# A four-segment attention block with FFN on one core: values of segment 0 in column strips, its first FFN matmul in 64-row tiles, segment 2's FFN in general PSUM banks, VectorE products split off

## Chip, cores and metric

The kernel runs on one core of a Trainium2 chip. The metric is device time in microseconds (us) of one execution; a time is the median of several runs. The engines are TensorE (PE; its weight loads are listed apart as PEld), VectorE (DVE), ScalarE (ACT), GpSimd (POOL) and SyncE (SP), which issues nearly all DMAs. Each has its own queue and runs it in order.

## The reference, cut to what matters

```python
# x: [1, 2048, 576] bf16; 32 heads of 18; N = 4 segments of L = 512; F = 4608
h  = x + A(layernorm(x))
h2 = h + gelu(layernorm(h) @ w1 + b1) @ w2 + b2

def A(x):
    q, k, v = x @ wq, x @ wk, x @ wv            # split in heads and segments
    M, z = 0, 0
    for s in range(4):
        p     = softmax(qs @ ks.T * scale + mask)
        a_dot = p @ vs
        a_mem = phi(qs) @ M / (phi(qs) @ z + 1e-6)
        outs.append(g * a_mem + (1 - g) * a_dot)  # g = sigmoid(beta), per head
        M += phi(ks).T @ vs ;  z += sum(phi(ks))
    return concat(outs) @ wo
```

In segment 0 the memory is still empty, so only the softmax part is computed there. `mask` adds -1e9 (in bf16) where `ar[:, None] < ar[None, :]`; the kernel sets those weights to nought after the exponential.

## The kernel before, in words

**Order.** The program is a list of about 1,740 small operations ("ops"). Each has a name made of a stage tag and a kind (`A1exp`, `C00F1`), the engine it runs on, and a place in one overall order: both come from the table `TIMETABLE`, in which a row such as `"A00exp": "a 94 113"` says that the two ops of that name go to ScalarE at places 94 and 113 (letters p, a, d, g, s for TensorE, ScalarE, VectorE, GpSimd, SyncE). `schedule()` sorts the ops by place and gives buffers out in that order; so the order of every engine's queue, that of the DMAs on SyncE among them, is written out by hand. The costs in `add(...)` only choose which buffer of a pool is taken.

**Stages.** For each segment s of 512 tokens (4 tiles of 128):
- X: load x, layernorm (`layernorm`: statistics on VectorE, the power -0.5 on GpSimd, subtract and scale on VectorE), transpose. Segment 0 is transposed by TensorE, the others are written to `xnd` in DRAM and read back by a transposing DMA ("flip").
- P: projections q, k, v in halves of 288 columns into one PSUM bank each, evicted by VectorE or ScalarE ("copy"); q and k go to DRAM (`qkst`) and come back transposed (`A0flip`, `A1flip`, ...).
- M: the memory update (`M`, `macc`, `mblk`).
- A: scores in four 32-row tiles (`st0` in segment 0, `st` in the others) into `st`, the single score buffer of four banks; one exponential of 128x2048 on ScalarE (`exp`); masks on VectorE or GpSimd; values (`val`). In segments 1 to 3 the value matmul has v (19 columns) as its stationary operand in column strips of 32, the weights streaming, and the result is turned by VectorE (`valT`), divided (`comb`) and added to the memory part (`mem`, `memT`, `memfin`, `comb2`); `oT` turns the sum for the output projection. In segment 0 (`stage_A0`, lines 885 to 993) the value matmul has the weights `pt` as stationary operand (128x128) and v streaming, 19 columns each; the result has tokens on partitions, is divided in `comb`, brought into the order of the output projection by GpSimd (`perm`), and turned by TensorE (`T`) for tiles 0 and 1, by a DMA for tiles 2 and 3.
- B: output projection (`Po`), residual (`hadd`), second layernorm, transposed again into `x2T` (`B00T`, `B01T` on TensorE for the first two tiles of segment 0, DMA for all others).
- C: first FFN matmul (`F1`), bias, gelu. D: second FFN matmul (`F2`), residual, output.

**The first FFN matmul.** In segments 1 to 3 the contraction of 576 is cut into nine blocks of 64 rows; two row tiles of the array work side by side on two outputs, and `xn2` carries a copy of its first 64 columns behind its end (`tail`), so that the odd blocks can be transposed too. In segment 0 the contraction is cut into five blocks of 128 (the last one of 65, whose last row is one and carries the bias), over 256 tokens at a time (`C00`, `C01`), two outputs to a PSUM bank. Segments 0 and 1 evict to `hT` and then apply the gelu in batches; segments 2 and 3 (`s >= DIRECT`, which is 2) use four banks of their own, `late_s`, that come free when the score buffer is closed, and ScalarE applies the gelu straight from PSUM, one output at a time (line 1192).

**Buffers.** Four general PSUM banks `c_s` serve projections, values, transposes, F1 of segments 0 and 1 and all of F2. `x2T` of segments 1 to 3 is one buffer, `xd_s`, that lies over the two buffers of `xT_s`.

Of the kernel before, what the change touches and what calls it, by code (L numbers as in the profile page):

```python
# [24 lines left out]
    "A00T": "p 172",  # L25
    "A00comb": "d 142 148",
    "A00copy": "d 177",
    "A00exp": "a 94 113",
    "A00mask": "g 114 105 124 136",
    "A00perm": "g 155",  # L30
    "A00st0": "p 88 107",
    "A00val": "p 137 140 143 144",
    "A01T": "p 233",
    "A01comb": "d 181 220",
    "A01copy": "d 240",
    "A01exp": "a 134 151 174 198",
    "A01mask": "d154 g146 g182 g196",
    "A01perm": "g 229",
    "A01st0": "p 129 147 170 190",
    "A01val": "p 158 159 163 164 199 210 216 208",  # L40
    "A02comb": "d 406 466",
    "A02dma": "s 477",
    "A02exp": "a 343 370 358 383 429 397",
    "A02mask": "g 362 371 405 396",
    "A02perm": "g 470",
    "A02st0": "p 340 366 353 380 423 394",
    "A02val": "p 369 377 379 402 372 373 420 430 460 464 446 421",
    "A03comb": "d 322 351",
    "A03dma": "s 386",
    "A03exp": "a 239 269 254 224 286 328 298 312",  # L50
    "A03flip": "s 518",
    "A03mask": "g 249 257 293 303",
    "A03opad": "g 545",
    "A03perm": "g 355",
    "A03st0": "p 235 265 251 218 282 325 295 308",
    "A03val": "p 258 274 314 281 263 275 271 278 311 341 347 339 348 323 333 326",
    "A0flip": "s 96 85 127 119 184 192 202 231",
    "A1comb": "d 555 589 673 686 740 764 817 846",
    "A1comb2": "g570 g640 g680 g720 g744 d779 g820 g850",
    "A1eg": "a 445 475 565 652 581 696 710 768",  # L60
    "A1exp": "a 452 482 468 544 496 568 586 601 623 638 656 689 678 703 731 721 776 791 822 758",
    "A1flip": "s 417 426 503 527 495 542 600 716",
    "A1mask": "g512 g514 g499 g489 g553 g562 g506 g513 g618 g602 g612 g624 g660 g647 g648 g663 d707 g705 g697 g702 g708 g728 g748 g738 g774 g809 d785 g801 "
        "d819 d836 g769 d793",
    "A1mem": "p 517 532 655 692 617 759 733 780",
    "A1memT": "d 521 534 659 709 622 761 743 823",
    "A1memfin": "d 564 636 677 714 690 762 790 838",
    "A1oT": "d 695 799 826 858 856",
    "A1pq": "d 459 485 632 665 590 747 719 777",
    "A1rg": "g 438 449 548 604 556 711 682 750",  # L70
    "A1st": "p 447 478 465 530 492 563 582 595 614 634 651 687 670 698 727 717 770 786 812 751",
    "A1val": "p 528 579 631 674 712 753 810 840",
    "A1valT": "d 538 584 654 684 725 757 813 844",
    "A2comb": "d 947 998 984 1028 1049 1078 1135 1159",
    "A2comb2": "g951 d1013 g988 g1040 d1057 d1085 g1138 g1160",
    "A2eg": "a 835 784 907 954 999 985 1042 1058",
    "A2exp": "a 863 842 876 853 899 930 946 915 961 975 990 1015 1026 1006 1046 1064 1074 1104 1089 1132",
    "A2flip": "s 797 658 816 804 948 890 1025 970",
    "A2mask": "g881 d848 g854 g886 g896 g916 g919 g908 d950 d955 g963 d938 g935 g972 d987 g992 g1007 g1034 d1024 g1030 g1033 g1062 g1051 g1052 d1111 g1109 "
        "g1080 d1113 g1140 g1097 g1144 g1148",  # L80
    "A2mem": "p 845 855 952 981 1039 1016 1073 1103",
    "A2memT": "d 852 864 959 997 1048 1019 1076 1106",
    "A2memfin": "d 893 965 979 1009 1054 1079 1128 1139",
    "A2oT": "d 1043 1117 1095 1168 1169",
    "A2pq": "d 841 829 941 962 1003 1011 1060 1087",
    "A2rg": "g 828 825 891 832 968 995 1044 1055",
    "A2st": "p 860 839 872 849 892 927 942 910 957 971 986 1012 1022 1004 1035 1059 1072 1100 1081 1122",
    "A2val": "p 894 925 967 1001 1041 1069 1124 1150",
    "A2valT": "d 900 994 973 1021 1047 1077 1127 1155",
    "A3comb": "d 1221 1253 1299 1323 1374 1388 1416 1427",  # L90
    "A3comb2": "g1225 g1257 d1309 d1332 g1377 g1392 d1422 d1429",
    "A3eg": "a 1096 1170 1226 1161 1290 1337 1351 1370",
    "A3exp": "a 1146 1157 1167 1175 1231 1254 1269 1210 1295 1281 1319 1307 1329 1343 1355 1365 1375 1384 1396 1411",
    "A3flip": "s 1002 1133 1094 1107 1230 1166 1296 1301",
    "A3mask": "d1158 g1165 d1180 g1176 g1171 g1239 g1235 g1243 d1270 d1283 g1277 d1245 g1249 g1303 d1292 g1308 g1325 g1320 d1335 d1339 g1338 d1363 g1366 "
        "g1361 d1371 g1397 d1391 d1399 g1402 g1412 g1419 d1420",
    "A3mem": "p 1145 1224 1247 1276 1310 1347 1390 1389",
    "A3memT": "d 1147 1228 1258 1279 1311 1359 1407 1394",
# [186 lines left out]
    "omg": "g 81",  # L285
    "ones": "a 213 166",
    "tri": "g 66",
    "warm": "p 5 14 20 24",
    "x1": "a 2",
}  # L290

# [109 lines left out]
def kernel(  # L401
# [13 lines left out]
    P = 128  # L415
# [1035 lines left out]
```

## Time and profile before

| | us |
|---|---|
| median of 3 runs (lowest, highest) | 457.35 (456.49, 458.07) |
| the profiled execution | 457.92 |
| its span, first to last instruction | 456.2 |
| granted clock of TensorE | 1.00 |

The profile lists busy time by engine, then by source line. A duration there runs from an instruction's start to its modelled end; neighbours on one engine overlap, so the time that one takes from its engine is read from one start to the next. "1276 PE MATMUL" is the second FFN matmul, 1187 the row-tiled first one, 1225 that of segment 0, 754 the projections, 919 and 944 scores and values of segment 0, 1048 and 1074 those of segments 1 to 3.

```profile
L1187 PE MATMUL ps_l<-xreg,w1g 64*128 64x512 bf16 x648 | 70.5, 376 | 0.0
L1225 PE MATMUL ps_c<-xreg,w1g 128*128 128x256 bf16 x288 | 40.9, 272 | 0.3 <-DMA w1g<-in_B_w_dram 0.3
L944 PE MATMUL ps_c<-v_aug,pt 128*128 128x19 bf16 x320 | 12.2, 172 | 0.2
L1074 PE MATMUL ps_c<-pt,v_aug 128*19 128x512 bf16 x96 | 9.5, 385 | 0.7 <-DVE qk_pad L599 0.3 <-DVE t L1029 0.3
```

### The profile page before, as it was taken

What the parts mean: (1) busy time and instruction counts of PE and PEld (TensorE: products, weight loads), DVE (VectorE), ACT (ScalarE), POOL (GpSimd) and SP (SyncE); (2) the same over time, 40 slices, a digit from 0 to 9 for tenths busy, and PEclk for the clock granted to TensorE, in tenths of its full rate; (3) what the DMA queues carried; (4) which work ended last, traced back from release to release, by engine and by line L of the source; (5) the groups of instructions that cost most, each with busy time, mean ns of one, the idle gap of its engine ahead of it and who ended that gap; (6) DMA issues with size and microseconds to landing.
All of it is one profiled execution on the core that took longest, in us unless ns stands there. A gap on an engine that the chain in (4) does not pass through costs nothing.

```text
span 456.2 us, 11278 instructions
## 1 busy us (share of the span) xinstructions
PE 443.6 (97%) x4721; PEld 290.2 (64%) x4721; DVE 282.5 (62%) x653; ACT 300.8 (66%) x285; POOL 148.6 (33%) x226
## 2 busy tenths in 40 slices
PE   7988999999999999999999999999999999999997
PEld 3766788866667766664444566565446776445775
DVE  6897899898878888887888789795201202000111
ACT  4878889998879885677899987853663002664000
POOL 4655544262645334635314266340100201000100
PEclk9999999999999999999999999999999999999999
DMA  7999999997969995693781615584560354450121
GB/s 240 245 240 221 283 292 260 254 245 219 243 195 278 311 237 149 150 218 83 209 190 28 202 32 86 89 215 129 172 223 25 126 121 150 154 157 1 41 78 40
DMA packets 82067, 77.91 MB, mean 171 GB/s; under 512 B 59232, under 2 KB 69216, under 8 KB 82016
## 3 DMA queue, kind: packets, MB, share of 16 engines
q1 hardware_dynamic: 81872, 77.04, 63.1%
q8 instruction: 37, 0.61, 0.6%
q10 hardware_dynamic: 144, 0.15, 0.1%
q14 instruction: 14, 0.11, 0.1%
HBM read 43.62 MB, written 19.53 MB: 138 GB/s over the span
## 4 chain that ended last, share of the span: by engine, by line
PE 83%; ACT 5%; DMA 5%; DVE 3%; SPq 1%; issue 1%; POOL 0%; ACTq 0%; DVEq 0%
PE ps_c L1276 30%; PE ps_l L1187 15%; PE ps_c L754 12%; PE ps_c L1225 8%; PE ps_c L1187 6%; PE st L1048 4%; ACT pt L1052 3%; PE ps_c L1074 2%; DMA w1g<-in_B_w_dram 1%; ACT hT L1207 1%; PE ps_c L944 1%; DMA hT<-in_A_w_dram 1%; DMA xreg<-xnd 1%; SPq L586 1%; PE ps_c L1026 1%
## 5 line engine op out<-in xcount | busy, mean ns | idle before, releaser
L1276 PEld LDWEIGHTS <-hT 128*128 128x128 bf16 x1152 | 110.0, 98 | 34.8 <-issue 7.4
L1052 ACT ACTIVATE pt<-st 128x2048 bf16<-128x2048 f32 x60 | 112.6, 1877 | 27.8 <-PE st L1048 22.3
L1192 ACT ACTIVATE hT<-ps_l,b_col 128x512 bf16<-128x512 f32 x72 | 45.2, 684 | 70.7 <-PE ps_l L1187 70.7
L1187 PEld LDWEIGHTS <-w1g 64*128 64x128 bf16 x972 | 46.7, 94 | 57.1 <-issue 3.3
L1276 PE MATMUL ps_c<-w,hT 128*128 128x288 bf16 x576 | 77.8, 286 | 0.0
L1276 PE MATMUL ps_c<-w_lo,hT 128*128 128x288 bf16 x576 | 77.6, 286 | 0.0
L1187 PE MATMUL ps_l<-xreg,w1g 64*128 64x512 bf16 x648 | 70.5, 376 | 0.0
L1288 DVE TENSOR_TENSOR ot<-ps_c,hc 128x288 bf16<-128x288 f32 x32 | 13.8, 449 | 85.9 <-PE ps_c L1276 76.2
L1063 POOL TENSOR_SCALAR_AFFINE_SELECT pt<-pt 128x512 bf16<-128x512 bf16 x70 | 48.8, 712 | 51.6 <-ACT pt L1052 51.6
L754 PE MATMUL ps_c<-hT,xreg 128*128 128x288 bf16 (+1 forms) x440 | 61.2, 286 | 1.3 <-DMA xreg<-xnd 1.2
L754 PEld LDWEIGHTS <-xreg 128*128 128x128 bf16 (+1 forms) x440 | 40.5, 97 | 13.9 <-issue 1.9
L1225 PE MATMUL ps_c<-xreg,w1g 128*128 128x256 bf16 (+1 forms) x360 | 43.6, 272 | 0.3 <-DMA w1g<-in_B_w_dram 0.3
L923 ACT ACTIVATE pt<-st 128x2048 bf16<-128x2048 f32 x20 | 37.6, 1878 | 5.9 <-PE st L919 4.6
L1225 PEld LDWEIGHTS <-w1g 128*128 128x128 bf16 (+1 forms) x360 | 34.0, 97 | 6.8 <-issue 1.1
L675 POOL TENSOR_TENSOR ln<-ln,mhalf 128x1 f32<-128x1 f32 x32 | 19.3, 606 | 57.5 <-DVE ln L672 56.8
L1187 PE MATMUL ps_c<-xreg,w1g 64*128 64x512 bf16 x324 | 37.2, 377 | 0.0
L1262 POOL TENSOR_TENSOR hc<-hc,b_bc 128x576 f32<-128x576 f32 x11 | 14.4, 1308 | 68.0 <-DMA hc<-hd 68.0
L1122 DVE TENSOR_TENSOR h<-ps_c,xb 128x288 f32<-128x288 f32 x32 | 13.5, 452 | 36.1 <-PE ps_c L754 31.9
L1090 POOL TENSOR_TENSOR o_nat<-t,t 128x288 bf16<-128x288 f32 x16 | 14.6, 914 | 39.6 <-DVE t L1087 31.9
L1048 PE MATMUL st<-qk 32*128 32x512 bf16 (+3 forms) x384 | 23.8, 300 | 1.9 <-ACT pt L1052 1.9
L1202 DVE TENSOR_SCALAR hT<-ps_c,b_col 128x512 bf16<-128x512 f32 x25 | 17.9, 743 | 6.9 <-PE ps_c L1187 6.7
L754 PE MATMUL ps_c<-wt_o,oT 128*128 128x288 bf16 x160 | 22.1, 286 | 0.0
(115 smaller groups left out, 553.7 us busy)
## 6 DMA issues: line engine op xcount, KB each, us to landing
w1g<-in_B_w1d_dram SPq DMA_DIRECT2D x27, 576.0 KB, 4.0
w1g<-in_B_w_dram SPq DMA_DIRECT2D x15, 640.0 KB, 6.1
qkd<-qk_pad SPq DMA_DIRECT2D x15, 512.0 KB, 4.9
hd<-h SPq DMA_DIRECT2D x16, 288.0 KB, 3.8
hc<-hd SPq DMA_DIRECT2D x16, 288.0 KB, 3.1
w_lo<-in_B_w_dram SPq DMA_DIRECT2D x3, 864.0 KB, 5.4
w<-in_B_w_dram SPq DMA_DIRECT2D x3, 864.0 KB, 7.4
xb<-in_A_x_dram SPq DMA_DIRECT2D x16, 144.0 KB, 4.1
```

Of the source, the lines that this page charges most:

```text
L675: nc.gpsimd.tensor_tensor(out=sm.t[:, 15:16], in0=sm.t[:, 14:15], in1=mhalf[:], op=ALU.pow)
L754: nc.tensor.matmul(out=c.t[:, 0:HALF], lhsT=xTb.t[0:kk, k, ts], rhs=wt[0:kk, hf, k, :], start=(k == 0), stop=(k == 4))
L923: ex = add(ps, {"act": 1.88}, lambda e, st=st, pt=pt: nc.scalar.activation(out=pt.t[:], in_=st.t[:], func=ACT.Exp, scale=scale), [sc], pt, ...
L1048: nc.tensor.matmul(out=st.t[:, i, off:off + n_], lhsT=qk[rows, 1, kt * P:(kt + 1) * P], rhs=qk[rows, 0, kt * P:L], start=True, stop=True, ...
L1052: ex = add(ps, {"act": 1.88}, lambda e, st=st, pt=pt: nc.scalar.activation(out=pt.t[:], in_=st.t[:], func=ACT.Exp, scale=scale), [sc], pt, ...
L1063: nc.gpsimd.affine_select(out=blk, in_=blk, pattern=[[0, 4], [1, P]], compare_op=ALU.is_ge, fill=0.0, base=0, channel_multiplier=-1)
L1090: a = add(pc, {"dve": 0.75, "pool": 0.94}, lambda e, g=g, t1=t1: VEC[e].tensor_tensor(out=o_q(on)[:, :, Dh * g:Dh * g + Dh], in0=t1.t[:, : ...
L1187: nc.tensor.matmul(out=cc[w].t[:], lhsT=wv[rows, k, q, :], rhs=x2T[s].t[rows, k, :], start=(k == 0), stop=(k == ND - 1))
L1192: ready_f[f + w] = [add(pf - 12, {"act": 0.68}, lambda e, f=f, w=w, cc=cc: nc.scalar.activation(out=hT[:, :, f + w, :], in_=cc[w].t[:].rea ...
L1202: nc.vector.tensor_scalar(out=dst, in0=src, scalar1=b, scalar2=None, op0=ALU.add)
L1225: nc.tensor.matmul(out=c.t[:, u * n_:(u + 1) * n_], lhsT=w1.t[0:kk, k, j * P:(j + 1) * P], rhs=x2T[s].t[0:kk, k, ts], start=(k == 0), stop ...
L1276: nc.tensor.matmul(out=c.t[:, 0:HALF], lhsT=hT[:, tl // 2, f, (tl % 2) * P:(tl % 2 + 1) * P], rhs=w2_c[ch][:, f - ch * WCH, hf * HALF:(hf ...
```

## The change

1. Segment 0's attention (`stage_A0`) is rewritten in the manner of the other segments: v is the stationary operand in column strips, a bank holds two groups of four heads by 256 tokens; VectorE turns the bank (`valT`), takes the reciprocal and multiplies by 1 - g (`rec`), GpSimd multiplies (`comb`) into `o_nat`, VectorE turns that into `oT`. The GpSimd `perm`, the TensorE transposes of `o_nat`, the DRAM tile `od` and its transposing load go. Scores of tokens 256 to 511 go in matmuls of 256 columns, eight to a step; there are 20 steps and exponentials as before.
2. The first FFN matmul of segment 0 is cut into nine blocks of 64 rows in two row tiles, 256 tokens at a time, four outputs in two banks per op; the bias is added in the eviction. `xn2` gets its tail in segment 0 too, and the odd blocks are transposed as well (by TensorE for tiles 0 and 1, by a second DMA for 2 and 3). Only the paired form of w1 is loaded.
3. `DIRECT` goes from 2 to 3: segment 2's F1 uses the general banks, with evictions (`C2copy`) and three gelu batches. `HALVES` goes from (18, 36) to (20, 36).
4. `x2T` gets two places in turn, one over `xT_s` (segments 1 and 3), one behind it (0 and 2).
5. VectorE ops are split: the addition of epsilon moves to GpSimd, ahead of the power; `memfin` becomes a reciprocal (`rec`) and a product that can go to GpSimd (17 of 24 do); `tail` can go to VectorE (6 of 12 in segments 1 to 3 do).
6. The whole timetable is written anew.

The timetable, a few of its rows (before, after):

```diff
-    "A0flip": "s 96 85 127 119 184 192 202 231",
+    "A0flip": "s 82 95 106 111 171 180 265 253",
-    "A03st0": "p 235 265 251 218 282 325 295 308",
-    "A02st0": "p 340 366 353 380 423 394",
+    "A02st0": "p 208 225 243 258 276 292 313",
+    "A03st0": "p 330 348 358 376 390 401 419",
-    "M0mblk": "d 364",
+    "M0mblk": "d 188",
-    "P1copy": "a195 d241 a234 d227 d236 a191 d179 a185 d204 a211 a219 d206 d290 a381 d349 d319 d400 d463 a262 d273 a266 d342 a248 a378",
+    "P1copy": "a173 a192 a230 a226 a222 d249 a177 a203 a202 a199 a196 a194 a289 a296 d315 a311 a347 d342 a241 a245 a264 a293 a277 a274",
-    "X1flip": "s 139 207",
+    "X1flip": "s 125 190",
-    "C2gelu1": "a 1436 1446 1443 1437 1471 1470 1463 1464 1483 1481 1477 1475 1486 1485 1490 1489 1493 1492 1498 1496 1501 1502 1505 1506 1514 1512 1509 1508 "
+    "C2gelu": "a 1482 1515 1532",
...
```

The code:

```diff
-    DIRECT = 2
-    HALVES = (18, 36)
+    DIRECT = 3
+    HALVES = (20, 36)
...
-    xreg = const.tile([P, 3, KT, L], BF16, name="xreg")
-    x2_s = Slots([xreg[:, 2, :, :]])
-    xd_s = Slots([xreg[:].rearrange("p j k t -> p (j k) t")[:, 0:ND, :]])
+    xreg = const.tile([P, 2 * KT + ND, L], BF16, name="xreg")
+    x2_s = Slots([xreg[:, 0:ND, :], xreg[:, 2 * KT:2 * KT + ND, :]])
...
-                nc.vector.tensor_scalar(out=sm.t[:, 14:15], in0=sm.t[:, 13:14], scalar1=EPS, scalar2=None, op0=ALU.add)
             def rstd(e):
+                nc.gpsimd.tensor_scalar(out=sm.t[:, 14:15], in0=sm.t[:, 13:14], scalar1=EPS, scalar2=None, op0=ALU.add)
                 nc.gpsimd.tensor_tensor(out=sm.t[:, 15:16], in0=sm.t[:, 14:15], in1=mhalf[:], op=ALU.pow)
...
+            def values(tag, t0, parts, banks, acq, cost):
+                units = [u for p_ in parts for u in p_[0]]
+                def fn(e):
+                    for (g, kt, q0, n_, off, pt) in units:
+                        o = banks[g // 2].t
+                        c0 = (g % 2) * 2 * P + q0 - t0
+                        for i in range(4):
+                            nc.tensor.matmul(out=o[32 * i:32 * i + Dh + 1, c0:c0 + n_], lhsT=va[kt][:, 4 * g + i, :], rhs=pt.t[:, i, off:off + n_],
+                                             start=fresh, stop=False, tile_position=(0, 32 * i), skip_group_check=True)
...
+            def finish(tag, p, gp, bank, val):
+                a = add(prio - 0.2, {"dve": 0.70}, lambda e: nc.vector.transpose(out=t1.t[:].rearrange("p a b -> p (a b)"), in_=bank.t[:]),
+                        [val], t1, [bank], name="valT")
+                def c0(e):
+                    nc.vector.reciprocal(out=r1.t[:], in_=t1.t[:, :, Dh])
+                    nc.vector.tensor_tensor(out=r1.t[:]..., in0=r1.t[:]..., in1=omg_q[:, 2 * gp:2 * gp + 2]..., op=ALU.mult)
+                def c1(e):
+                    VEC[e].tensor_tensor(out=o_q(on)[:, 8 * p:8 * p + 8, ...]..., in0=t1.t[:, :, 0:Dh]..., in1=r1.t[:]..., op=ALU.mult)
+                a = add(prio - 0.2, {"dve": 0.48}, c0, [a] + later, r1, [t1], name="rec")
+                return add(prio - 0.2, {"dve": 0.52, "pool": 0.95}, c1, [a], None, [r1, t1, on], name="comb")
...
+            first = [step("A00", Q, [(b, 0, 0, P, b * P) for b in range(4)]) for Q in range(2)]
+            for Q in range(2):
+                parts = [first[Q]] + [step("A01", Q, [(b, kt, P, P, b * P) for b in range(4)]) for kt in (1, 0)]
+                banks = {2 * Q: Buf(c_s), 2 * Q + 1: Buf(c_s)}
+                v = values("A01", 0, parts, banks, True, 1.25)
+                cs += [finish("A01", 0, gp, banks[gp], v) for gp in (2 * Q, 2 * Q + 1)]
+            turn("A01", 0, cs)
+            for Q in range(2):
+                s0, s1 = two(0, 0), two(0, 1)
+                s3 = step(f"A0{2 + Q}", Q, [(b, 3, 3 * P, P, b * P) for b in range(4)])
+                for b in (0, 2):
+                    if b:
+                        s0, s1 = two(b, 0), two(b, 1)
+                    s2 = two(b, 2)
+                    gp = 2 * Q + b // 2
+                    banks = {gp: Buf(c_s)}
+                    values(f"A0{2 + Q}", 2 * P, [s0, s1], banks, True, 0.45)
+                    v = values(f"A0{2 + Q}", 2 * P, [s2, k3], banks, False, 0.43)
+                    cs.append(finish(f"A0{2 + Q}", 1, gp, banks[gp], v))
+            turn("A03", 1, cs)
...
+                rc = add(pg + 0.01, {"dve": 0.25}, lambda e, t2=t2, r2=r2: nc.vector.reciprocal(out=r2.t[:], in_=t2.t[:, :, Dh]), [mt], r2, [t2], name="rec")
                 def fin(e, t2=t2, r2=r2):
-                    nc.vector.reciprocal(out=r2.t[:], in_=t2.t[:, :, Dh])
-                    nc.vector.tensor_tensor(out=t2.t[:, :, 0:Dh], in0=t2.t[:, :, 0:Dh], in1=r2.t[:]..., op=ALU.mult)
-                t2_ok[g] = add(pg + 0.01, {"dve": 0.80}, fin, [mt], r2, [t2], name="memfin")
+                    VEC[e].tensor_tensor(out=t2.t[:, :, 0:Dh], in0=t2.t[:, :, 0:Dh], in1=r2.t[:]..., op=ALU.mult)
+                t2_ok[g] = add(pg + 0.01, {"dve": 0.56, "pool": 0.95}, fin, [rc], None, [t2, r2], name="memfin")
...
-                            for u in range(nf):
-                                for k in range(KT):
-                                    kk = KTAIL if k == 4 else P
-                                    nc.tensor.matmul(out=c.t[:, u * n_:(u + 1) * n_], lhsT=w1.t[0:kk, k, j * P:(j + 1) * P], rhs=x2T[s].t[0:kk, k, ts],
-                                                     start=(k == 0), stop=(k == 4))
+                        for q in range(2):
+                            for k in range(ND):
+                                for w in range(2):
+                                    rows = slice(64 * w, 64 * w + 64)
+                                    nc.tensor.matmul(out=cc[w].t[:, q * 2 * P:(q + 1) * 2 * P], lhsT=w1.t[rows, k, q, :], rhs=x2T[s].t[rows, k, ts],
+                                                     start=(k == 0), stop=(k == ND - 1))
...
+                        def evict(e, f=f, w=w, c=cc[w], half=half):
+                            if e == "act":
+                                for q in range(2):
+                                    nc.scalar.activation(out=dst[:, q, :], in_=src[:, q, :], func=ACT.Identity, bias=b[:, q:q + 1])
+                            else:
+                                nc.vector.tensor_tensor(out=dst, in0=src, in1=b.unsqueeze(2).to_broadcast([P, 2, 2 * P]), op=ALU.add)
...
```

## The prediction

> **What bounds it now.** I read the page first: busy shares, the clock row, the chain.
>
> ```profile
> PE 443.6 (97%) x4721; PEld 290.2 (64%) x4721; DVE 282.5 (62%) x653; ACT 300.8 (66%) x285; POOL 148.6 (33%) x226
> PEclk9999999999999999999999999999999999999999
> PE 83%; ACT 5%; DMA 5%; DVE 3%; SPq 1%; issue 1%; POOL 0%; ACTq 0%; DVEq 0%
> ```
>
> TensorE is busy 97% of the span at full clock and holds 83% of the chain, so work taken off TensorE counts one for one until another engine is as full. Busy times of TensorE overlap (ends are modelled), so I price by starts in the timeline, from one group to the next.
>
> ```profile
> 59.71 0.40 PE L919 MATMUL st<-w_lo,qk 32*128 32x128 bf16 x16
> 60.04 0.36 PE L944 MATMUL ps_c<-v_aug,pt 128*128 128x19 bf16 x8
> 60.26 1.26 PE L1225 MATMUL ps_c<-xreg,w1g 128*128 128x256 bf16 x10
> 61.35 0.35 PE L944 MATMUL ps_c<-v_aug,pt 128*128 128x19 bf16 x8
> 61.56 0.77 PE L754 MATMUL ps_c<-hT,xreg 128*128 128x288 bf16 x5
> ...
> 206.00 4.06 PE L1187 MATMUL ps_c<-xreg,w1g 64*128 64x512 bf16 x36
> 209.99 0.40 PE L1048 MATMUL st<-qk 32*128 32x384 bf16 x8
> 210.64 0.72 PE L1074 MATMUL ps_c<-pt,v_aug 128*19 128x512 bf16 x16
> 211.29 1.04 PE L1187 MATMUL ps_c<-xreg,w1g 64*128 64x512 bf16 x8
> ```
>
> So a score step takes 0.33 us, eight old value matmuls 0.21, ten first-FFN matmuls of segment 0 1.09, 36 row-tiled ones of 512 columns 3.99, the 16 column-strip value matmuls of one later group 0.65. Then the waits: 18.10 to 56.95 holds the first thirteen score starts, 239.24 to 290.52 most of segment 3's.
>
> ```profile
> 18.10:56.95 38.85, 36.06 (x597) 28.21 (x596) 32.26 (x100) 32.13 (x35) 22.81 (x30) 1.00 1.03 242
> 239.24:290.52 51.28, 49.18 (x503) 29.57 (x503) 43.45 (x93) 46.99 (x30) 24.35 (x37) 1.00 0.35 85
> 300.00:453.10 153.10, 153.08 (x1347) 96.01 (x1346) 29.60 (x67) 48.77 (x75) 10.13 (x15) 1.00 0.39 116
> ...
> PE ps_c L856 <- DVE oq L958: 1.4, 1, 1.4
> PE ps_c L754 <- DMA xreg<-xnd: 1.2, 1, 1.2
> PE st L1048 <- ACT pt L1052: 1.9, 5, 0.6
> ```
>
> Columns: span, then busy PE, PEld, DVE, ACT, POOL. The last window is pure TensorE; the first two hold the waits. Slot by slot (start to start above the usual slot) I get 3.5 us lost in the first window and 4.1 in the second.
>
> **The change, part by part.** *First FFN matmul of segment 0.* Before: 36 groups x 1.09 = 39.2 us. After: 18 groups of 36 matmuls of 256 columns, two row tiles side by side, 18 pairs each. A 256-column matmul has a slot of 0.109, a pair at that slot gives 18 x 0.109 = 1.96, times 18 = 35.3: minus 3.9 us. The trace has no 64-row matmul of 256 columns. Lower bound: this slot. Upper bound: the two weight loads of a pair don't overlap; the load row has 94 ns each, so 188 per pair, 18 x 18 x 0.188 = 60.9, plus 21.7. I take the lower end: in the score step 16 loads of 32x128 and their matmuls fit into 0.33, 21 ns each, and a 128x128 load with a 19-column matmul into 0.21 / 8 = 26 ns; 94 is latency.
>
> *Values of segment 0.* Before: 320 matmuls in 40 groups x 0.21 = 8.4. After, columns per strip: twice 12 x 128, four times 4 x 256, four times 2 x 256 + 2 x 128; together 10,240. The later segments' group streams 1,280 columns per strip in 0.65, 0.56 without the 0.09 of the change of form, or 0.44 ns a column: 4.5. Minus 3.9; I keep 3.7, the groups being shorter. Bounds: 0.42 ns a column (4.3) and the full 0.65 per 1,280 (5.2).
>
> *Transposes.* Ten of `o_nat` go, eight odd-half ones of `xn2` come, 0.06 each: minus 0.1.
>
> *Changes of form.* Twenty L1225 matmuls take 2.30 before a score and 2.20 before other full-array work: 0.09 per change between full, row-tiled and strip form. In the TensorE entries of the timetables I count 199 changes before and 219 after (values and segment 0's F1 now differ from their neighbours): plus 1.9. TensorE's work falls by 3.9 + 3.7 + 0.1 - 1.9 = **5.8 us**.
>
> *The first stage.* All four engines have to run through it. VectorE and ScalarE instructions also overlap by some 0.1:
>
> ```profile
> 18.63 1.89 ACT L923 ACTIVATE pt<-st 128x2048 bf16<-128x2048 f32 x1
> 20.40 0.69 ACT L828 ACTIVATE ek<-qk_pad 128x576 bf16<-128x576 bf16 x1
> 20.97 0.40 ACT L595 CAST qk_pad<-ps_c 128x288 bf16<-128x288 f32 x1
> ```
>
> 1.77 for an exp, 0.57 for `ek`, 0.28 for a copy. With such slots I add up what each timetable puts between the first and the thirteenth exp. Before: TensorE 35.3, ScalarE 29.9, VectorE 29.8, GpSimd 20.3, in 38.85 us. After: TensorE 33.7, ScalarE 32.9 (20 copies of P1 instead of nine), VectorE 34.2 (five bank transposes at 0.63, four `rec`, five `oT`, `M0mblk` moved up here), GpSimd 26.0. Three engines are level, so waits must grow: I take 5 us instead of 3.5, plus **1.5**; bounds 0 (time 37.2) and plus 8.5 (TensorE down to 74% of the stage). Queues: P01's qk stores stand ahead of the two transposing loads that the A02 scores need, and X1's second one is issued right behind these (before: behind three); it landed at 44.2, 6 us after its issue at 38.2, and held TensorE 1.2. Its first user now comes 2.6 us of TensorE work earlier, its queue is one load (1.3) shorter, so that wait stays, inside the 5.
>
> *Segment 3's scores.* One score buffer: an exp starts 0.45 after its score and takes 1.88, so scores less than 2.4 apart wait. Before, the order puts 1.30, 2.37, 2.37, 2.12, 2.04, 2.13 and 2.33 us of TensorE work between neighbours; after, no two of segment 3 are closer than 2.63 (five of the first stage are, at 2.2 to 2.3: part of the 5). Of the 4.1, some 0.6 for bank waits and 1.5 behind the 2.8 to 7.0 us gelu batches stay: minus **2.0**, bounds 0 and minus 3.5.
>
> *Costed at nothing.* The epsilon add goes from VectorE (0.154) to GpSimd, which has no 128x1 add in the trace; between its memset of 128x1 (0.1) and its power (0.55) per layernorm; the chain behind it ends 20 us of TensorE work before the F1 that needs it. Without that cover it is four in a row, 0.4 to 2.2 per segment. `memfin` on GpSimd (0.86 by L1090 instead of 0.46) in 17 of 24 cases: `comb2`, behind it, waits for values anyway; uncovered, the last one adds 0.4 per segment. Evictions of segment 0's F1 on ScalarE are two of 256: between 0.69 (one of 512) and 1.01 (two of 128x288 with a scale, 0.507), seven instead of eleven of 0.58, ScalarE even within 1 us. Segment 2's 36 gelus of 0.68 become 36 evictions and three batches; VectorE is 29.6 busy in the last 153 us, ScalarE 48.8, and a pair of banks drains in 2 x 0.74 under a 1.94 us group. If not, each group waits 0.1 to 0.5. Its last batch (2.8 plus a table load of 1.3) has six F2 chunks of 0.74 ahead of its user. Loads shrink from 640 to 576 KB.
>
> [...]
>
> **Sum.** 457.92 (this execution: span 456.2 and 1.7 around it) - 5.8 + 1.5 - 2.0 = 451.6; the median is 457.35, 0.6 lower, so **451.1 us**. Start (first score at 18.1) and tail (last matmul to end 3 us) stay.
>
> **Rivals.** (1) Most of the saving is lost in the first stage: GpSimd and VectorE alternate in `rec`, `comb`, `oT`, TensorE waits for banks. For: three engines within 1.5 us of each other. Against: from 60 to 140 us TensorE runs at 19.6 to 20 of 20 with ScalarE at 16 to 18.7. At plus 6.5 instead of 1.5: 456.1; 0.16. (2) Slower: the weight loads of the 64-row pairs show. Place: 324 pairs in segment 0. It decides once a pair takes over 0.109 + (458.7 - 451.1) / 324 = 0.132 us (458.7 is 0.3% above the median); fully serial it gives 451.1 + 25.6 = 476.7. Against: 21 and 26 ns above. 0.06. (3) Slower by the same stage at its upper bound, with nothing won in segment 3: 451.1 + 7 + 2 = 460.1; 0.08. (4) The stage costs nothing and segment 3 gives 3.5: 448.1; 0.12. Forecast (448.8 to 454.5): 0.58.
>
> 0.3% (1.4 us) is about what a measurement of this kernel tells from no change: faster is under 456.0, slower over 458.7. Faster: 0.58 + 0.12 + half of (1), 0.08, less 0.02 for the forecast's own edge = 0.76. Slower: (2) and (3), 0.14, less 0.02 where their price is small = 0.12. Same: the other 0.08 of (1) and these two times 0.02 = 0.12. The range takes case (4) below and (1) above: 447.5 to 457.0.
>
> **What will show it.** Right: segment 0's F1 group of 36 at 1.96 start to start; strip values 0.67, 0.45 and 0.34; the thirteenth score 38 to 40 us after the first; no wait of `st` for `pt` in segment 3; PE from 300 us on as full as now. Wrong: a pair over 0.12; a thirteenth score later than 42 us after the first; waits of F1 for `hT` evictions in segment 2; waits of F2 for a gelu batch.

## The result, and the profile after

The changed kernel takes 455.88 us (median of 20 runs, 453.31 to 458.87); the kernel before took 458.21 beside it (20 runs, 456.49 to 459.85). The ratio is 0.995, 95% interval 0.9928 to 0.9973: faster by half a per cent, where 451.1 us, or 1.4%, was forecast. The range held the time; the size was missed by two thirds.

The profiled execution took 457.12 us, with a span of 455.4 and a mean granted clock of 0.992. The clock matters for reading every number below: of the 20 runs, the eight with a mean clock of 0.993 or less have a median of 457.4, the twelve others 454.0. The clock is not all of it: two of the twelve, both at 0.996, took 457.86 and 458.87.

From the page of the changed kernel: busy time by engine, the clock in 40 slices, the chain's shares by engine.

```profile
PE 441.5 (97%) x4815; PEld 280.5 (62%) x4815; DVE 288.6 (63%) x638; ACT 305.0 (67%) x275; POOL 172.8 (38%) x270
PEclk9999997999999999999999999999999999999999
PE 78%; DVE 8%; DMA 4%; ACT 4%; POOL 3%; issue 2%; SPq 0%; DVEq 0%; ACTq 0%; POOLq 0%
```

The clock row was 9 throughout; now its seventh slice (68.3 to 79.7 us) shows 7. TensorE's share of the chain fell from 83 to 78%: it waits more, and for several engines.

The windows that answer to the three of before, chosen by the same events, and two around the dark slice (columns as before: us, busy PE, PEld, DVE, ACT, POOL, then the clock, the DMA share, GB/s):

```profile
15.89:56.50 40.61, 35.88 (x525) 24.82 (x526) 36.84 (x108) 35.85 (x48) 30.39 (x50) 1.00 0.92 236
69.00:72.42 3.42, 1.32 (x32) 0.77 (x26) 1.17 (x3) 2.79 (x4) 1.21 (x3) 1.00 1.06 213
73.29:79.24 5.95, 5.95 (x47) 3.18 (x49) 3.33 (x11) 1.69 (x3) 2.13 (x4) 0.50 1.16 249
237.91:289.00 51.09, 51.01 (x514) 30.87 (x509) 38.54 (x82) 43.55 (x29) 22.50 (x34) 1.00 0.54 138
300.00:452.30 152.30, 152.01 (x1339) 94.44 (x1337) 44.45 (x90) 57.42 (x60) 15.21 (x22) 1.00 0.35 105
```

Segment 3's window is full now: 51.01 of 51.09. The tail is full as well. The first thirteen scores take 40.61 us instead of 38.85; but they begin at 15.89 us instead of 18.10, a start that the forecast left where it was, so the thirteenth still comes 0.45 us earlier than before. And from 73.29 us on TensorE runs at half clock for 5.95 us.

TensorE's timeline across the dark slice (start, us, line, operands, count; in brackets the idle time before the first of the group and what ended it), and the DMA queue that SyncE feeds:

```profile
67.19 2.14 PE L1244 MATMUL ps_c<-xreg,w1g 64*128 64x256 bf16 x36
69.27 0.72 PE L854 MATMUL ps_c<-v_aug,fk_pad 128*128 128x76 bf16 x16
69.92 0.40 PE L920 MATMUL st<-w_lo 32*128 32x256 bf16 x8
73.29 3.78 PE L752 MATMUL ps_c<-hT,xreg 128*128 128x288 bf16 x15 [2.97 <-DMA xreg<-xnd]
```

```profile
55.29 1.26 SPq L577 DMA_DIRECT2D xnd<-xn  x2
59.03 2.28 SPq L577 DMA_DIRECT2D w1g<-in_B_w_dram  x2
61.41 0.37 SPq L819 DMA_DIRECT2D qkd<-qk_pad  x1
61.89 6.88 SPq L584 DMA_TRANSPOSE xreg<-xnd  x1
```

The 15 products at 73.29 are the first that read X2. Their transposing load is issued at 61.89, behind two loads of first-FFN weights (576 KB each) that had to wait until 59.03 and 60.97 for the product groups ahead to free a buffer, and lands 11.4 us later, at 73.25. In the kernel before, the same load went out later than that and landed earlier, 7.3 us after its issue, at 72.0; its first user came at 74.2 there, and here TensorE was ready for it at 70.25:

```profile
64.65 5.25 SPq L586 DMA_TRANSPOSE xreg<-xnd  x1
```

So of 2.2 us to spare before, the earlier user took 4.0 and the later landing 1.3. The 15 products of the changed kernel then take 3.71 us to the next group, where 15 slots at full clock take 1.95.

To see where all the time went I add up every start on TensorE that comes more than 0.15 us later than its usual slot, by stretch of the span:

| part | forecast | found |
|---|---|---|
| TensorE's work | -5.8 | -4.9 |
| late starts before 16 us | 0 | -0.8 (3.8 to 3.0) |
| late starts 16 to 58 us | +1.5 | +3.3 (3.4 to 6.7) |
| late starts 58 to 100 us | 0 | +3.7 (0.5 to 4.2; X2's load 3.1) |
| slower slots at half clock, beyond these | 0 | +1.7 |
| late starts after 100 us | -2.0 | -4.0 (5.6 to 1.6) |
| sum | -6.3 | -1.0 |

The first row is start to last matmul less the late starts: 438.2 before, and 433.2 to 433.6 in three executions at full clock (of runs told below) whose TensorE does the same work. In the changed kernel's own execution it is 435.0; the 1.7 above 433.3 is the half clock's. The last matmul starts 1.1 us earlier than before; as the first row is what the others leave, the sum has to come out at that. How much goes to which row depends on what is called the usual slot: by the profile's own list of TensorE's waits, the row from 16 to 58 us is +1.9 (2.6 to 4.5) and the row after 100 us -2.7 (3.1 to 0.4).

### The profile page after: what moved, and what is told of

It reads as the page before. It is cut to its first block, busy times and chain, and to the rows that moved or that the text cites. A ratio compares the mean times of both kernels' runs of the same rounds, so it can differ in the third digit from the quotient of the medians.

```text
span 455.4 us, 11480 instructions
## 1 busy us (share of the span) xinstructions
PE 441.5 (97%) x4815; PEld 280.5 (62%) x4815; DVE 288.6 (63%) x638; ACT 305.0 (67%) x275; POOL 172.8 (38%) x270
## 4 chain that ended last, share of the span: by engine, by line
PE 78%; DVE 8%; DMA 4%; ACT 4%; POOL 3%; issue 2%; SPq 0%; DVEq 0%; ACTq 0%; POOLq 0%
PE ps_c L1294 29%; PE ps_c L1207 13%; PE ps_c L752 12%; PE ps_l L1207 8%; PE ps_c L1244 5%; PE st L1071 4%; PE ps_c L1097 3%; DMA xreg<-xnd 2%; ACT hT L1227 1%; PE ps_c L1048 1%; DMA hT<-in_A_w_dram 1%; DVE ln L668 1%; ACT pt L1075 1%; POOL pt L936 1%; DVE xn L683 1%
## 5 line engine op out<-in xcount | busy, mean ns | idle before, releaser
L1207 PEld LDWEIGHTS <-w1g 64*128 64x128 bf16 x972 | 46.7, 94 | 56.8 <-issue 4.1
L1207 PE MATMUL ps_c<-xreg,w1g 64*128 64x512 bf16 x648 | 73.4, 376 | 0.0
L1086 POOL TENSOR_SCALAR_AFFINE_SELECT pt<-pt 128x512 bf16<-128x512 bf16 x68 | 47.8, 716 | 51.4 <-ACT pt L1075 51.3
L1212 ACT ACTIVATE hT<-ps_l,b_col 128x512 bf16<-128x512 f32 x36 | 22.8, 684 | 45.7 <-PE ps_l L1207 45.7
L1222 DVE TENSOR_SCALAR hT<-ps_c,b_col 128x512 bf16<-128x512 f32 x46 | 33.0, 744 | 13.8 <-PE ps_c L1207 13.6
L1244 PE MATMUL ps_c<-xreg,w1g 64*128 64x256 bf16 x648 | 38.2, 271 | 0.1
L1207 PE MATMUL ps_l<-xreg,w1g 64*128 64x512 bf16 x324 | 35.1, 376 | 0.0
L1244 PEld LDWEIGHTS <-w1g 64*128 64x128 bf16 x648 | 30.8, 95 | 6.8 <-issue 3.1
L1227 ACT ACTIVATE hT<-hT 128x8192 bf16<-128x8192 bf16 (+2 forms) x6 | 32.0, 5326 | 0.1
L1220 ACT ACTIVATE hT<-ps_c,b_col 128x512 bf16<-128x512 f32 x26 | 17.2, 687 | 16.2 <-PE ps_c L1207 16.0
L1255 DVE TENSOR_TENSOR hT<-ps_c,b_col 128x512 bf16<-128x512 f32 x29 | 19.2, 679 | 7.1 <-PE ps_c L1244 7.1
```

The costliest lines, as they stand in the source:

```text
L1086: nc.gpsimd.affine_select(out=blk, in_=blk, pattern=[[0, 4], [1, P]], compare_op=ALU.is_ge, fill=0.0, base=0, channel_multiplier=-1)
L1207: nc.tensor.matmul(out=cc[w].t[:], lhsT=w1.t[rows, k, q, :], rhs=x2T[s].t[rows, k, :], start=(k == 0), stop=(k == ND - 1))
L1212: ready_f[f + w] = [add(pf - 12, {"act": 0.68}, lambda e, f=f, w=w, cc=cc: nc.scalar.activation(out=hT[:, :, f + w, :], in_=cc[w].t[:].rea ...
L1222: nc.vector.tensor_scalar(out=dst, in0=src, scalar1=b, scalar2=None, op0=ALU.add)
L1227: ge = add(2.9, {"act": 0.40 * (f1 - f0) + 0.25}, lambda e, f0=f0, f1=f1: nc.scalar.activation(out=hT[:, :, f0:f1, :], in_=hT[:, :, f0:f1, ...
L1244: nc.tensor.matmul(out=cc[w].t[:, q * 2 * P:(q + 1) * 2 * P], lhsT=w1.t[rows, k, q, :], rhs=x2T[s].t[rows, k, ts], start=(k == 0), stop=(k ...
```

## The experiments

Theory **T1**: the loss is X2's load, 3 us late, and the half clock that the idle time brings. Rival **T2**: the engines that share the first stage are level, so what is saved there returns as other waits. Rival **T3**: the idle time alone counts, the clock is a mark of it. Each run is set against runs of the kernel before on the same chip.

**X2's load first.**

```diff
-    "X2flip": "s 339",
+    "X2flip": "s 305.5",
```

> The changed kernel with one place of its timetable altered: the load that brings X2 in transposed is issued directly after the last store of X2's rows, ahead of two loads of first-FFN weights and of a store of q and k that stand before it in the changed kernel. Theory T1: the changed kernel lost its saving at one point, where TensorE stood idle for 3.0 us at 70.3 us for this load and the granted clock then fell to 0.5 for 6.8 us, together about 6 us. It expects the idle time at that point under 0.5 us, no slice of the clock row below 9 after the first 10 us, a mean granted clock of 1.000, and 449 to 451.5 us, 1.4 to 2.0% below the kernel before. Rival T2 (the three engines that share the first 57 us are so evenly loaded that what TensorE saves there comes back as other waits): TensorE waits for something else instead, within 15 us of the same point, and the time stays at 453 to 457. Rival T3 (the idle time alone counts, the clock is a mark of it and no cost of its own): 452 to 453.5. The weight loads behind it come some 3 us later, and 2 us of new idle at the first FFN product would be T2's.

453.59 us (12 runs), ratio 0.9919 (0.9895 to 0.9942). T1's 449 to 451.5 was missed; the time lies in T2's 453 to 457. SyncE's queue and TensorE of this run:

```profile
58.87 2.70 SPq L584 DMA_TRANSPOSE xreg<-xnd  x1
61.66 1.00 SPq L577 DMA_DIRECT2D w1g<-in_B_w_dram  x2
```

```profile
66.75 0.40 PE L920 MATMUL st<-w_lo 32*128 32x128 bf16 x16
69.08 3.75 PE L1244 MATMUL ps_c<-xreg,w1g 64*128 64x256 bf16 x36 [1.93 <-DMA w1g<-in_B_w_dram]
```

The wait for X2 is gone. The weights, now issued 2.6 us later, are late in its place: 1.93 us, and the 36 products behind it run slow (3.69 us to the next group, 2.07 at full clock). So the wait moved one transfer on. That is T2's shape, but at a place that can be mended: one queue, three transfers, each order making another one late.

**X2's load in halves.** The code that splits X1's load is used for X2 too.

```diff
-                if s == 1:
+                if s in (1, 2):
...
-    "X2flip": "s 339",
+    "X2flip": "s 300 305.5",
```

> The changed kernel with X2's transposing load made as two, of 256 tokens each, as X1's is: the first half is issued as soon as its own two stores allow, before the stores of the second half; the second directly after these. T1 expects no idle time at X2's first projection and the same 449 to 451.5 us as with the whole load issued early; one more transposing load on the queue may cost the loads behind it 1 to 2 us, which T1 expects to lie hidden. T2: 453 to 457.

454.53 us (6 runs), 0.992 (0.9894 to 0.9946); clock 0.993 in the profiled execution. T1's time was missed again. The first half goes out at 55.55 us, ahead of the stores of the second half's rows, which follow at 57.13; the second half at 60.37; the weights at 61.75. The same first-FFN group waits 3.38 us, with half clock for 6.8 us behind it:

```profile
70.78 4.02 PE L1244 MATMUL ps_c<-xreg,w1g 64*128 64x256 bf16 x36 [3.38 <-DMA w1g<-in_B_w_dram]
```

**The same wait, but not idle.**

```diff
+            dummies = 24 if (gr.tag, nm, tl, hf) == ("P2", "k", 0, 0) else 0
             def fn(e):
+                for _ in range(dummies):
+                    nc.tensor.matmul(out=c.t[:, 0:HALF], lhsT=warm[:, 0:P], rhs=warm[:, 0:HALF], start=True, stop=True)
```

> The changed kernel with 24 products of 288 columns added ahead of X2's first projection, on operands that are there, into the bank that the projection then starts afresh: work that no result uses, 24 x 0.122 = 2.9 us, in the 3.0 us for which TensorE waits. The load still lands at 73.3 us, so the wait is as long as it was; only the idleness is taken away. T1 expects the clock to stay at 1.0, X2's first 15 products to take 0.12 us each where they took 0.24, and the time to fall by 2.5 to 3.5 us against the profiled 457.1 of the changed kernel, to 453 to 454.5. T3, by which the lower clock costs nothing of its own: no gain, 456 to 457 with the wait.

455.02 us (6 runs), 0.9937 (0.9914 to 0.9960): 0.5 above the window of T1, and too near the changed kernel's own 0.995 for the times to decide. The timeline decides about the products:

```profile
71.10 3.11 PE L752 MATMUL ps_c<-pt 128*128 128x288 bf16 x24
74.05 2.01 PE L755 MATMUL ps_c<-hT,xreg 128*128 128x288 bf16 x15
```

The 24 fill the wait (the trace names their operands after tiles that share the memory), and X2's 15 take 2.01 us where they took 3.78. In this execution the clock fell elsewhere, for 3.41 us at 30 us, behind the waits at 28 us that the changed kernel also has.

**The kernel before, made late.** Its own load of X2 goes behind two stores; then the same with work in the wait.

```diff
-    "X2flip": "s 354",
+    "X2flip": "s 387",
```

> The kernel before with its own transposing load of X2 issued later, behind a store of q and k and a store of segment 0's output rows, so that it lands at 76 to 78 us in place of 70 and TensorE must wait for it 2 to 4 us at the first product of X2. T1 expects the clock row of the kernel before, which is 9 throughout, to get a slice below 9 near 75 us, and the time to grow by the idle time and about 3 us more: 4.5 to 7 us, 463 to 465. T3 expects the idle time alone: 460 to 462. If TensorE waits under 1.5 us the run says nothing of either.

464.03 us (6 runs), 1.012 (1.010 to 1.0139): 5.9 above the kernel before, inside T1's window and above T3's.

```diff
     "X2flip": "s 387",
...
+            dummies = 34 if (gr.tag, nm, tl, hf) == ("P2", "v", 1, 0) else 0
```

> The kernel before with X2's transposing load late, as in the run that gave 464.03, and 34 products of 288 columns on data that is there (34 x 0.122 = 4.15 us) ahead of the first product that needs X2, in the 4.2 us that TensorE stood idle. Their result is used by nothing. The load is as late as it was. T1: the clock stays at 1.0 after the wait, where it was 0.5 for 6.8 us, and the time falls by 2.5 to 3.5 us, to 460.5 to 461.5. T3 (the idle time alone counts): 463.5 to 464.5.

461.87 us (4 runs), 1.0103 (1.0074 to 1.0132); 0.4 above T1's window and 1.6 below T3's. Both windows were reckoned from a kernel before at 458.17 us; beside this run it took 457.21, and with the windows moved down by that 1.0 us the time lies 1.4 above the one and 0.6 below the other. The two ratios overlap: by times alone the price of the clock is 0.8 us (the ratios) to 1.2 us (each median against its own kernel before), not T1's 2.5 to 3.5, and not sure. The timelines of the late kernel and of the one with work show the same step as above:

```profile
78.40 1.38 PE L754 MATMUL ps_c<-hT,xreg 128*128 128x288 bf16 x5 [4.01 <-DMA xreg<-xnd]
```

```profile
75.98 4.33 PE L754 MATMUL ps_c<-pt 128*128 128x288 bf16 x34 [0.81 <-POOL pt L938]
80.15 0.78 PE L757 MATMUL ps_c<-hT,xreg 128*128 128x288 bf16 x5
```

Five products of X2 take 1.38 us after 4 us of idleness and 0.78 after 4.2 us of useless work. T3 is refuted for the products. For a whole run the price of the half clock stays open: 0.6 to 0.9 us by the first pair (in which not every execution met it), 0.8 to 1.2 by the second, and 3.4 by the changed kernel's 20 runs split by clock, a split that shows what goes together and not what causes it.

**Each transfer in the order of its use.** The fourth load of weights goes first, X2's load second, the fifth load third; the fourth and fifth product groups change places, since the fifth load had the earlier user.

```diff
-    "C00F1": "p 320 316 349 392 361 427 442 436 487",
+    "C00F1": "p 320 316 349 361 392 427 442 436 487",
-    "X2flip": "s 339",
+    "X2flip": "s 325.5",
```

(The four eviction places of these two groups in `C00copy` are exchanged with them.)

> The changed kernel with three transfers in another order and two first-FFN groups exchanged: the fourth load of first-FFN weights goes out first (as soon as the buffer is free, at 59 us), then X2's transposing load, then the fifth load; the product groups of the fourth and fifth load change places, so that the earlier load has the earlier user. Theory T1, as the runs before have left it: with X2's load put first the wait went to the weights (1.9 to 3.5 us at 67 us) and with the weights first it is at X2 (3.0 us at 70 us), since one queue carries all three and each order makes one late; the work has room for all of them when each comes in the order of its use. It expects no idle time of TensorE over 0.7 us between 60 and 85 us, a granted clock of 1.0 there, and 450.5 to 452.5 us. Rival T2 (DMA has too much to carry there in any order): 1.5 to 3 us idle again somewhere from 60 to 80 us, and 453 to 456.

452.80 us (6 runs, 452.00 to 454.63), 0.9906 (0.9879 to 0.9933); the mean clock is 0.999 or 1.000 in all six. The time is 0.3 us above T1's 450.5 to 452.5. Queue and TensorE:

```profile
59.61 0.34 SPq L577 DMA_DIRECT2D w1g<-in_B_w_dram  x1
60.12 4.63 SPq L584 DMA_TRANSPOSE xreg<-xnd  x1
64.81 0.57 SPq L577 DMA_DIRECT2D w1g<-in_B_w_dram  x1
```

```profile
67.66 2.14 PE L1244 MATMUL ps_c<-xreg,w1g 64*128 64x256 bf16 x36
69.73 0.72 PE L854 MATMUL ps_c<-v_aug,fk_pad 128*128 128x76 bf16 x16
70.39 0.40 PE L920 MATMUL st<-w_lo 32*128 32x256 bf16 x8
70.72 2.02 PE L752 MATMUL ps_c<-hT,xreg 128*128 128x288 bf16 x15
```

No gap, with the same three transfers and the same products. By the ratios, 0.9950 and 0.9906, this is worth 2.0 us; the medians differ by 3.1, but the kernel before took 458.21 us beside the one and 457.21 beside the other. The two intervals still touch (0.9928 and 0.9933), so it is the timeline that shows the wait gone. T1's cause holds for this place, and the DMA was not too full, only wrongly ordered. One new wait of 1.15 us comes at 83.0 us, for a bank that VectorE has not emptied; T1 had expected none over 0.7.

**The first stage's own waits.** On top of that order, four copies on GpSimd go behind the masks that they delayed, and two loads of q and k go ahead of the output weights.

```diff
-    "A0flip": "s 82 95 106 111 171 180 265 253",
+    "A0flip": "s 82 95 106 111 165.3 165.6 265 253",
-    "omg": "g 123",
+    "omg": "g 146.5",
```

> The kernel with the three transfers in the order of their use, and two more places altered for the first 40 us: the four small copies on GpSimd that spread the gates (1.06 us) go behind two causal masks of the second query tile instead of ahead of them, and the two transposing loads that bring the q and k of segment 0's later half go ahead of the load of the output weights. In the changed kernel TensorE waits 1.8 us at 27 to 29 us for those masks and 1.3 to 1.6 us at 37 us for the first of these loads. T1 (each of the waits is a matter of the order on one queue, not of an engine that is full): both go, by 2.0 to 3.0 us in sum, the clock stays at 1.0 in the slice near 28 us, and the time is 448 to 450. T2 (in the first 57 us the engines are level, so a wait taken away returns elsewhere): under 1 us of gain against the kernel with the transfers' order alone.

453.48 us (10 runs), 0.9921 (0.9897 to 0.9945): nothing gained, and T1's 448 to 450 missed. T2 is right here. The waits of TensorE from 15 to 60 us, in the changed kernel and in this one (what waited, for what, us in total, times, longest):

```profile
PE st L920 <- DMA w_lo<-qkd: 1.3, 1, 1.3
PE ps_c L952 <- POOL pt L936: 1.1, 1, 1.1
PE ps_c L752 <- DVE t L966: 0.6, 1, 0.6
```

```profile
PE ps_c L752 <- DVE t L966: 2.1, 1, 2.1
PE ps_c L854 <- DVE fk_pad L830: 0.9, 1, 0.9
```

The load and the masks are no longer waited for. VectorE is: 0.6 became 2.1. In front of the transpose of line 966 it works off segment 0's memory block, and not at its own speed. VectorE of the changed kernel, and GpSimd at that time:

```profile
34.59 0.99 DVE L873 TENSOR_TENSOR MZ_blk<-MZacc,gmzm 32x144 bf16<-32x144 f32 x1
35.50 1.07 DVE L875 TENSOR_SCALAR MZ_blk<-MZacc,maskcol,epscol 32x8 bf16<-32x8 f32 x1
...
38.47 0.30 DVE L873 TENSOR_TENSOR MZ_blk<-MZacc,gmzm 32x144 bf16<-32x144 f32 x1
```

```profile
34.32 2.22 POOL L936 TENSOR_SCALAR_AFFINE_SELECT pt<-pt 128x1024 bf16<-128x1024 bf16 x2
```

The operation of line 873 takes 0.99 us while GpSimd masks, and 0.30 at 38.47, behind the masks; the whole block, eight operations (the next expectation miscounts them as twelve), takes 4.4 us, where eight at 0.30 are 2.4.

**The block moved out of the stage**, and the seventh and eighth product groups exchanged (with their evictions), on top of the transfers in the order of use, once with the places of the run above and once without:

```diff
-    "C00F1": "p 320 316 349 361 392 427 442 436 487",
+    "C00F1": "p 320 316 349 361 392 427 436 442 487",
-    "M0mblk": "d 188",
+    "M0mblk": "d 341.5",
```

> The kernel of the run that gave 453.48 (transfers in the order of their use, gate copies behind the masks, q and k ahead of the output weights), with two more places altered: the twelve VectorE operations that build segment 0's memory block (4.4 us at 34.7 us in that run, 2.6 us where GpSimd does not read beside them) go to where VectorE has idle time, near 60 us, ahead of the first accumulation of segment 1; and the seventh and eighth first-FFN groups change places, so that the load that was issued earlier is used earlier. In that run the two waits at 27 and 37 us had gone, but TensorE waited 2.1 us at 38.8 us for VectorE's transpose of a value bank, which stood behind the memory block. T1 (the waits are a matter of order): with the block moved nothing takes their place, the waits from 20 to 60 us fall from about 6 us to under 4, the 1.9 us at 83 us go, and the time is 448.5 to 450.5. T2 (the first stage's engines are level): another wait of 1.5 us or more before 60 us, and 451.5 to 453.5.

452.28 us (4 runs), 0.9877 (0.9859 to 0.9896). Late starts from 16 to 58 us fall to 4.9, not under 4, and T1's 448.5 to 450.5 was missed. T2's time fits; its wait of 1.5 us did not come. The block takes 2.43 us at its new place (expected were 2.6) instead of 4.4, the wait of 2.1 us for VectorE's transpose is gone, and the longest that is left before 60 us is 0.9.

> The kernel of the run that gave 452.80 (only the transfers near 60 us in the order of their use), with the memory block of segment 0 moved to near 60 us and the seventh and eighth first-FFN groups exchanged, but the gate copies and the loads of q and k where the changed kernel has them. The waits at 28 us (1.4 us, masks) and at 37.7 us (1.6 us, load) stay; the 0.7 us at 40.8 us for VectorE goes and the 1.3 us at 82.7 us goes. T1: 450.5 to 452. T2: 452 to 453.5.

451.94 us (4 runs, 451.29 to 453.14), 0.9871 (0.9851 to 0.9890): the fastest kernel here, its interval clear of the changed kernel's 0.9928 to 0.9973, and at the upper end of T1's window, 0.06 us from T2's. Late starts from 16 to 58 us are 4.4, where the changed kernel has 6.7; those of 83 us fell from 1.5 to 0.6. Not all of the 4.4 is the block's doing: in this execution the clock fell at 30.9 us for 3.41 us, and behind that the load at 37.7 us, whose place is as it was, is waited for by 0.2 us where 1.6 were expected. Moving masks and loads adds nothing to it: the two medians differ by 0.3 us, well inside the intervals. Against the run with the order alone the gain is 0.9 us by the medians and 1.6 by the ratios, the wait at 83 us is part of it, and the intervals overlap. That VectorE's block was the binding piece is shown by the wait of 2.1 us that went with it in the run before, not by the times.

**The products given to GpSimd.** The 17 of `memfin` go back to VectorE (`g` to `d` in the rows of `A1memfin` to `A3memfin`, all else as in the changed kernel).

```diff
-    "A3memfin": "d1220 g1255 g1290 d1345 g1370 g1374 d1416 g1437",
+    "A3memfin": "d1220 d1255 d1290 d1345 d1370 d1374 d1416 d1437",
```

> The changed kernel with all 24 products of the memory output with its reciprocal on VectorE, at the same places of the order, where 17 of them are on GpSimd. If the split of these products is what freed segment 3's scores (waits of 1.9 us for the exponentials' tiles in the kernel before, none in the changed one), 17 x 0.45 = 7.7 us more on VectorE brings 1 us or more of waits back between 236 and 292 us, and 456.5 to 458. If it is the new order and the other banks of segment 2's first FFN product, the waits stay away and the time is that of the changed kernel, 453.5 to 458 with its median near 455.9.

456.99 us (10 runs), 0.9985 (0.9959 to 1.0010): not told apart from the changed kernel, nor from the kernel before, and inside both of the windows expected. The waits decide: between 236 and 292 us TensorE waits for nothing in its profile either, so the split did not free segment 3's scores; the new order or the banks of segment 2's first FFN product did, which no run here separates. Its profile settled another point. X2's load is late by as much as in the changed kernel, but the clock does not fall:

```profile
73.84 2.02 PE L752 MATMUL ps_c<-hT,xreg 128*128 128x288 bf16 x15 [2.83 <-DMA xreg<-xnd]
```

The same wait, products at full speed, a mean clock of 1.000 and a span of 453.5 against 455.4. So the length of the wait alone does not decide about the clock; the last section says what goes with it.

## Why the prediction was off

**Cost of the strip forms: right.** An F1 group of 36 takes 2.07 us from its start to the next group, 0.09 of it the change of form: 1.98, forecast 1.96. A pair takes 0.109 us from start to start, the forecast's own slot and far from the 0.132 at which the rival of visible weight loads would have decided; that rival is refuted. The value groups take 0.55 and 0.44 with the change of form, so 0.46 and 0.35, forecast 0.45 and 0.34. TensorE's work fell by 4.9 rather than 5.8; the missing 0.9 I do not find in these groups, and leave it open; the 4.9 is what the late starts leave of the time, so it is no surer than their count.

**Segment 3: right in kind, too small.** No wait of `st` for `pt` is left, and the late starts after 100 us fell by 4.0 instead of 2.0. The 1.5 us that I left standing behind the gelu batches went too: by the profile's list, TensorE's waits from 80 us on fell from 3.4 us to 0.4.

**First stage: the mechanism right, the size too small.** Forecast were waits of 5 us and 38 to 40 us from first to thirteenth score; measured 6.7 and 40.6. The sentence that the start stays at 18.1 was wrong, to the good: the first score comes at 15.89. The three level engines were named. What was mis-sized is VectorE: I summed its slots at their uncontended length, with `M0mblk` among them, and added nothing for work that runs beside GpSimd's masks. The block moved up into the one stage without room and cost 4.4 us of VectorE instead of 2.4. Its operation of line 873, with two tensors as its inputs, takes 0.99 us beside the masks and 0.30 at 38.47; that of line 875, with one tensor and two columns, stretches as much, from 0.29 to 1.07. What stretches them is not shown. X1's second load, which I expected to be waited for still, is not; the wait of 1.3 us near there is for the q and k loads.

**The step that failed: nothing was said about X2's load.** The sum has no term for it, and "Loads shrink from 640 to 576 KB" is the only sentence that comes near. I followed X1's load along the queue and stopped there. X2's first user moved from place 399 to 377, and came 4.0 us earlier; the load, at 339, now stood behind two loads of weights that wait for a buffer of a product group at 320 and 316, and took 11.4 us to land instead of 7.3. With its half clock it cost 3.1 + 0.7 + 1.7 = 5.5 us of the changed kernel's profiled execution (0.7 are late starts between groups at half clock), about the whole forecast gain. Over all runs it is less, since not every execution pays for the clock: of the 6.3 us forecast, 2.3 came; by the ratios the order of use gives back 2.0, and the block with the exchange of two groups another 1.6. The run with all of these, 451.94 us, 0.9871, has the gain that the forecast's 451.1 (0.986 of 457.35) had asked for.

**The clock.** I read the clock row of before, all nines, as a property of the kernel. It was that of one execution. Of the 45 executions of the kernel before that were run beside the experiments, 22 have a mean clock of 0.993 to 0.996 and the others 0.999 or 1.000; 3.41 us at half clock lower the mean by 0.004 (0.996 in the profiled execution of the run with 24 products, which has one such interval). In both runs of the kernel before with X2's load late the clock also falls near 30 us, ahead of anything that was altered.

The likeliest rival, "most of the saving is lost in the first stage: 456.1", names nearly the right time for mostly the wrong place: the found sum is 5.3 us above the forecast one, to which the stretch of X2's load gives 5.4 and the first stage 1.8; the work that did not go gives 0.9, and segment 3 and the start take back 2.8.

## What to carry to other kernels

When an order written by hand changes, walk every transfer of every queue: what it waits for, what stands ahead of it, when it lands by a measured landing time, and when its first user now comes; here two loads that waited for a buffer until 59.03 and 60.97 us kept X2's load, behind them on the queue, until 61.89. A wait on TensorE can cost more than its length: behind 3.0 us of idleness the changed kernel's profiled execution lost another 2.4 at half clock. And in a stage where engines are level, sum their time with the stretched durations that the trace shows beside GpSimd's masks (0.99 us for 0.30 here), not with the medians.

## What the chip showed that I had not expected

In these traces the clock falls on a raster. In every profiled execution in which it falls between the first and the last matmul, once it is up, the intervals at half clock last 3.41 or 6.83 us, and the first of them begins a whole number of 3.413 us after the clock came up: 68.27 us after it in the changed kernel (20 of these periods), 64.85 in two runs (19), 37.55 in one (11), 23.89 in four (7). I laid this raster over TensorE's idle time, which a window row gives as its length less busy PE. The ten falls follow periods of 3.41 us with 1.4 to 2.4 us of idleness: the changed kernel at 70 us (2.1; the window 69.00 to 72.42 above, 1.32 us busy of 3.42), the first-FFN wait with X2's load first or in halves (1.9 each), the late load in the kernel before (2.4), both falls in the run with masks and loads moved (2.0 and 1.9), the waits at 28 us in four runs (1.4, 1.5, 1.6 and 1.8). Every period at full clock with more than 1.6 us of idleness was followed by half clock. Between 1.4 and 1.6 both occur, so idleness counted this way does not fix the line. In the run with `memfin` on VectorE the 2.83 us of idleness at 71.0 us is cut by a boundary at 72.60, and neither period is over 1.6:

```profile
69.19:72.60 3.41, 1.82 (x40) 1.21 (x36) 1.16 (x2) 2.32 (x3) 0.74 (x1) 1.00 1.06 210
72.60:76.02 3.42, 2.17 (x23) 1.59 (x27) 1.34 (x5) 1.10 (x3) 2.15 (x2) 1.00 1.16 257
```

The clock stays. The boundary cuts the wait at another point than in the changed kernel (1.6 us into it, at 72.60, there 2.1 us into it, at 72.42), and a wait of nearly the same length is followed by half clock in one run and not in the other; this goes with the changed kernel's spread of 5.6 us over 20 runs, without being shown to be all of it.

Nor does the length of a gap decide in these runs: one of 1.93 us, in the run with X2's load first, was followed by half clock where it fell into a single period, and one of 2.83 us, in the run with `memfin` on VectorE, was not where it fell into two.
